# Block-causal attention and FFN on one core: bfloat16 scale sums, leans per operation, and q-high by k-low scores in four 64x64 tiles

## Chip, core and metric

The kernel runs on one NeuronCore of a Trainium2 chip. TensorE (PE) does the matmuls and loads their weights (PEld), VectorE (DVE), ScalarE (ACT) and GpSimd (POOL) work on tiles in SBUF and PSUM, SyncE (SP) issues most of the DMAs and ACT the others. The metric is device time of one execution in microseconds; lower is better.

## The reference, cut

```python
def _attn_ref(q, k, v):                     # 8 batches, 8 heads, 576 tokens, 64 per head, float32
    scores = scale * np.matmul(q, k.transpose(0, 1, 3, 2))
    mask = block_i >= block_j               # blocks of 64 tokens: causal by block
    scores = np.where(mask, scores, -1000000000.0)
    scores = scores - np.max(scores, axis=-1, keepdims=True)
    attn = np.exp(scores)
    attn = attn / (np.sum(attn, axis=-1, keepdims=True) + 1e-09)
    return np.matmul(attn, v).astype(np.float32)

def _moe_ref(x, w_in, w_out):               # x: the heads side by side, 4608 x 512; d_ff 2048
    h = x @ w_in
    g = h * np.clip(h + 3.0, 0.0, 6.0) / 6.0
    return (g @ w_out).astype(np.float32)
```

## The kernel before

**Numbers in two halves.** From batch 1 on, every float32 operand of a matmul is scaled by a power of two and split into two float16 numbers, a high and a low one; a product is then three or four float16 products summed in PSUM. Batch 0 goes through float32 matmuls (names `qt`, `sf`, `pt`, `pr`, `pf`, and `h`, `o` of the first piece), because the weights are still being loaded and split then. The power of two comes from the largest absolute values: `pow2_scale` (L747) sums the 128 partitions' values with a matmul against a column of ones (`mb`, two instructions of 1 or 2 columns, float32), for q and k of each slot, for v of each batch and for five weight chunks (the last two through a transpose `mt` first); three more weight chunks have a sum of their own (`gs`, in `w_max`, L889).

**Slots.** A slot is one pair of heads of one batch; slots 0 to 3 are batch 0, slots 4 to 31 are batches 1 to 7. For a slot `qk_prep` (L1040) takes the absolute maxima `qkmx` (DVE; for the first slots ACT may do it), scales q and k, and lays out `qks` in three slices: q's high and low halves beside each other, k's high half twice, k's low half twice. One transposing DMA makes `qkT` of it: 128 rows, of which 64 are high and 64 low in slice 0.

**Scores.** `s_group` (L1289) computes the scores of three 64-token query blocks of a slot; three groups make the nine blocks. A 64-column tile of PE takes head 0 and the other 64-column tile head 1 (`128*64` in the profile: 128 rows by 64 columns), so instructions come in pairs that run side by side. Each block is two such pairs over its keys: q (high and low) by k high, and q (high and low) by k low. Group 1 has blocks of 256, 320 and 384 columns, each in a PSUM bank of its own; group 2 has 448, 512 and 576 (576 in two pieces, 64 of them beside the 448 in one bank, 512 in another). The score banks are the pool `ps_s`, three of them. After a bank DVE takes the row maxima (`st<-s`), scales them, ACT does the exponential with its sum (`p<-s`), and the result is split (`phl`), transposed by DMA (`pT`) and multiplied with v (`pv`).

**FFN.** Thirteen pieces of tokens go through `h` (w_in, 16 steps of a piece), `r` and `g` (ACT and DVE) and `o` (w_out), with up to four accumulators `o0` to `o3`; the last two pieces use a product with seven instead of eight submatrices (`m`). `ffn2_` (L1671) writes a piece's output tiles `osb` and their DMAs.

**Order.** Nothing is issued directly. A recorder notes every operation with its possible engines, and `schedule` (L474) lays them out with a model of costs, a due time for each and a table `SHIFT` of some 1,450 offsets to due times; `emit` (L677, line L681 in the profile) then issues them, so that all instructions have one line and tiles tell them apart. An operation with several possible engines goes to the one that would end first, with fixed handicaps (`BIAS`: 250 ns for DVE, 500 ns for POOL). PE works in the order it is given; matmuls of one `joint` group stay together.

Of the kernel before, what the change touches and what calls it, by code (L numbers as in the profile page):

```python
# [9 lines left out]
BF16 = mybir.dt.bfloat16  # L10
# [7 lines left out]
P = 128  # L18
# [33 lines left out]
QKA = 8  # L52
RDW = "PA"
# [1881 lines left out]
```

## Time and profile before

| what | us |
|---|---|
| median of 3 runs (992.11 to 992.73) | 992.53 |
| the profiled execution | 993.4 |
| its span on the core | 991.6 |
| PE busy (98%) | 971.2 |
| DVE busy (89%) | 883.6 |
| ACT busy (65%) | 641.9 |
| POOL busy (6%) | 58.7 |

The span runs from the first instruction to the last; 1.8 us of the profiled execution lie around it. Busy time of PE is the union of modelled matmul durations. A matmul's start is recorded, its end is modelled: what a stretch of matmuls costs is read from the start of its first to the start of the next stretch's first. PE's granted clock is full (1.00) throughout.

### The profile page before, as it was taken

How to read it: one execution, taken by the hardware profiler on the slowest of the kernel's cores; microseconds unless marked ns; L12 is line 12 of the kernel's file. 1: busy time of each engine (PE TensorE's matmuls, PEld its weight loads, DVE VectorE, ACT ScalarE, POOL GpSimd, SP SyncE). 2: the span in 40 equal slices, each digit the busy share in tenths (PEclk: the TensorE clock that was granted, in tenths of full speed). 3: DMA queues.
4: the chain of work that ended last, by engine and by line, in shares of the span. 5: the costliest groups of instructions: out<-in, count | busy, mean ns of one | idle time of the engine just before them, and what ended most of it. 6: DMA issues, size and time to landing. Idle time of an engine off the chain costs nothing.

```text
span 991.6 us, 31314 instructions
## 1 busy us (share of the span) xinstructions
PE 971.2 (98%) x12673; PEld 729.3 (74%) x12673; DVE 883.6 (89%) x2443; ACT 641.9 (65%) x1547; POOL 58.7 (6%) x228
## 2 busy tenths in 40 slices
PE   6899999999999999999999999999999999999998
PEld 5565667777768876777777777877777777887876
DVE  6898999999998999999999988898998879985863
ACT  4799777866756767676776656765766554444442
POOL 1132100000000000000000000000000000000000
PEclk9999999999999999999999999999999999999999
DMA  8975567999769999698888887576674452000000
GB/s 237 292 217 162 99 123 144 163 174 203 131 115 182 153 179 164 127 189 158 149 165 151 142 159 119 110 160 119 115 168 88 84 118 23 15 34 2 34 2 33
DMA packets 407041, 129.05 MB, mean 130 GB/s; under 512 B 393968, under 2 KB 396272, under 8 KB 406896
## 3 DMA queue, kind: packets, MB, share of 16 engines
q1 hardware_dynamic: 362816, 113.59, 58.8%
q10 hardware_dynamic: 44080, 13.46, 6.4%
q8 instruction: 99, 1.62, 0.7%
q14 instruction: 46, 0.38, 0.1%
HBM read 45.09 MB, written 9.44 MB: 55 GB/s over the span
## 4 chain that ended last, share of the span: by engine, by line
PE 46%; DVE 3%; ACT 1%; DMA 1%; issue 0%; ACTq 0%; DVEq 0%
PE o L681 21%; PE h L681 14%; PE m L681 6%; PE s L681 3%; PE pv L681 3%; DVE phl L681 1%; DVE st L681 1%; DVE g L681 1%; DMA vnat<-in_v_dram 1%; DVE r L681 0%; ACT p L681 0%; DVE x L681 0%; ACT r L681 0%; ACTq L681 0%; DVE vhl L681 0%
## 5 line engine op out<-in xcount | busy, mean ns | idle before, releaser
L681 PE MATMUL o<-wout,g 128*64 128x512 f16 (+3 forms) x3336 | 404.5, 379 | 0.0
L681 PE MATMUL h<-x,win 128*64 128x384 f16 (+2 forms) x3952 | 361.0, 319 | 2.1 <-DVE r L681 2.0
L681 PEld LDWEIGHTS <-win 128*64 128x64 f16 (+1 forms) x4440 | 271.8, 110 | 57.8 <-issue 4.7
L681 PEld LDWEIGHTS <-g 128*64 128x64 f16 x3360 | 221.6, 110 | 107.8
L681 ACT ACTIVATE p<-s,st,esc 128x64 f32<-128x64 f32 (+1 forms) x280 | 162.9, 587 | 58.9 <-DVE st L681 35.1
L681 ACT ACTIVATE r<-h,eg,sh 128x384 f32<-128x384 f32 (+1 forms) x192 | 111.4, 599 | 62.6 <-PE h L681 58.7
L681 DVE SCALAR_TENSOR_TENSOR phl<-p,st,phl 128x128 f16<-128x128 f32 (+4 forms) x252 | 136.0, 582 | 0.5 <-ACT phl L681 0.5
L681 DVE TENSOR_REDUCE st<-s 128x1 f32<-128x64 f32 (+2 forms) x280 | 117.8, 446 | 11.0 <-PE s L681 10.9
L681 ACT ACTIVATE g<-r 128x384 f16<-128x384 f32 (+1 forms) x153 | 77.7, 509 | 58.8 <-DVE r L681 39.9
L681 DVE SCALAR_TENSOR_TENSOR g<-r,g 128x384 f16<-128x384 f32 (+1 forms) x192 | 101.7, 534 | 13.4 <-ACT g L681 12.5
L681 DVE SCALAR_TENSOR_TENSOR r<-r,eg,h 128x384 f32<-128x384 f32 (+1 forms) x160 | 93.6, 586 | 10.3 <-ACT r L681 9.8
L681 PE MATMUL s<-qkT 128*64 128x512 f16 (+7 forms) x1120 | 96.8, 287 | 0.8 <-ACT p L681 0.3
L681 ACT ACTIVATE phl<-p,st 128x128 f16<-128x128 f32 (+4 forms) x135 | 71.9, 565 | 37.8 <-DVE st L681 23.1
L681 PEld LDWEIGHTS <-vhl 128*64 128x64 f16 x1680 | 72.0, 110 | 11.3 <-issue 3.6
L681 PEld LDWEIGHTS <-qkT 128*64 128x64 f16 x1120 | 59.6, 110 | 24.2 <-issue 5.0
L681 PE MATMUL pv<-pT,vhl 128*64 128x192 f16 (+2 forms) x1680 | 73.0, 233 | 2.3 <-DVE x L681 1.9
L681 ACT ACTIVATION_READ_ACCUMULATOR p<-s,st,esc 128x1 f32 x280 | 55.3, 197 | 0.0
L681 POOL MEMSET p<- 128x64 f32 x140 | 21.3, 152 | 556.0 <-DVE phl L681 519.1
L681 ACT ACTIVATE r<-hf,eg,sh 128x192 f32<-128x192 f32 (+1 forms) x48 | 25.8, 591 | 38.6 <-DVE hf L681 38.6
L681 DVE TENSOR_SCALAR phl<-p,st 128x384 f16<-128x384 f32 (+4 forms) x117 | 45.0, 413 | 1.3
L681 DVE SCALAR_TENSOR_TENSOR qks<-qk,rs_q,qks 128x576 f16<-128x576 f32 x56 | 44.5, 809 | 0.0
L681 PE MATMUL m<-x,ws 128*64 128x192 f16 x768 | 35.4, 246 | 0.0
(191 smaller groups left out, 1023.3 us busy)
## 6 DMA issues: line engine op xcount, KB each, us to landing
out_dram<-osb SPq DMA_DIRECT2D x35, 256.0 KB, 2.4
qk<-in_q_dram SPq DMA_DIRECT2D x23, 288.0 KB, 4.1
rawo<-in_moe_w_out_dram SPq DMA_DIRECT2D x12, 512.0 KB, 4.5
vnat<-in_v_dram ACTq DMA_DIRECT2D x34, 128.0 KB, 3.8
qk<-in_k_dram ACTq DMA_DIRECT2D x14, 288.0 KB, 4.8
qk<-in_k_dram SPq DMA_DIRECT2D x14, 288.0 KB, 4.3
vnat<-in_v_dram SPq DMA_DIRECT2D x30, 128.0 KB, 3.0
x<-in_moe_w_in_dram SPq DMA_DIRECT2D x7, 512.0 KB, 5.7
```

The costliest lines, as they stand in the source:

```text
L681: getattr(eng, method)(*args, **kw)
```

## The change

- **Scale sums.** The columns of ones become bfloat16, and the values summed are read as the upper 16 bits of their float32 words, in `pow2_scale` and `w_max`.
- **Scores in 64x64 tiles.** q's high and low words stand in swapped order in the odd blocks of 128 tokens of `qks`. In group 1 the 320-column block goes first, alone, then the 256- and 384-column blocks as one joint set in two banks; in group 2 the set of two banks stays as it was. In such a set q (high and low) by k high comes first, in 128x64 tiles. Then q high alone by k low, for two blocks and two heads, in four 64x64 tiles: the swap puts the two blocks' high words into different row halves. The product of the two low words is left out there (not in the other regions). Each such stretch, 56 of them, is four instructions.
- **qk_prep.** q's high words come from one instruction over ten blocks instead of nine, its low words from two DVE instructions (five and four blocks) instead of one. ACT may take the maxima `qkmx` in all slots.
- **Order.** `SHIFT` is another table; a new table `LEAN`, some 900 entries, adds to the handicap of DVE and POOL for single operations; POOL's costs in the planner are raised.
- **Small ones.** `rd` in `pv_group32` (batch 0) is one product on DVE or POOL instead of three on POOL or ACT. The last output tile is written in two halves, by ACT and DVE, with a DMA each. (`VMG` is 99, above every slot, so `v_max` is as before.)

```diff
-QKA = 8
-RDW = "PA"
+QKA = 32
+RDW = ("vector", "gpsimd")
+VMG = 99
...
-    0: -10, 2: 71, 3: -67, 4: -29, 5: 85, 6: -33, 7: -5, 8: 114, 11: -102, 12: 63, 13: 4, 14: -6, 15: 14,
...
+            op.lean = self.BIAS
+            if len(ways) > 1:
+                part = self.part[op.grp] = self.part.get(op.grp, -1) + 1
+                dv, dp = LEAN.get(10 * op.grp + part, (0, 0))
+                if dv or dp:
+                    op.lean = dict(vector=self.BIAS["vector"] + dv, gpsimd=self.BIAS["gpsimd"] + dp)
...
+    def upper(a):
+        return a.bitcast(BF16).rearrange("p (n w) -> p n w", w=2)[:, :, 1]
...
-            nc.tensor.matmul(ps[h * BLK:(h + 1) * BLK, :n], ones[:k_, :BLK], mx, start=True, stop=True)
+            nc.tensor.matmul(ps[h * BLK:(h + 1) * BLK, :n], ones[:k_, :BLK], upper(mx), start=True, stop=True)
...
-    one = wpool.tile([P, 1], F32, tag="one", name="one")
+    one = wpool.tile([P, 1], BF16, tag="one", name="one")
...
-        nc.scaled(sp[:, 0, :, 0], t[:, 0], rs[:, 0:1], "AV")
-        nc.scaled(sp[:, 1, :, 0], t[:, 1], rs[:, 1:2], "AV")
-        nc.vector.scalar_tensor_tensor(
-            sp[:, 0, :, 1], t[:, 0], rs[:, 0:1], sp[:, 0, :, 0], op0=ALU.mult, op1=ALU.subtract
-        )
+        nc.scaled(qs[:, :, 0::3], qf, rs[:, 0:1], "AV")
+        nc.scaled(sp[:, 2, :, 0], t[:, 1], rs[:, 1:2], "AV")
+        for u in range(2):
+            nc.vector.scalar_tensor_tensor(
+                sp[:, 0, u::2, 1 - u], t[:, 0, u::2], rs[:, 0:1], sp[:, 0, u::2, u],
+                op0=ALU.mult, op1=ALU.subtract,
+            )
...
-        for i in range(GB):
-            nc.scaled(rd[:, i], ident2, r[:, i:i + 1], RDW)
+        eye, rr = ident2.unsqueeze(1).to_broadcast([P, GB, BLK]), r.unsqueeze(2).to_broadcast([P, GB, BLK])
+        nc.add([(e, "tensor_tensor", (rd, eye, rr), dict(op=ALU.mult)) for e in RDW])
...
-            [[[(ii, 0, BLK * (GB + ii + 1), 0)]] for ii in range(GB)],
+            [[[(1, 0, 320, 0)]], [[(0, 0, 256, 0)], [(2, 0, 384, 0)]]],
...
+            pss = [ps_s.tile([P, 512], F32, tag="s", name=f"s{n}_{g}_{si}_{bi}") for bi in range(len(some))]
+            nc.joint = "s", n, g, si
+            work = []
             for bi, bank in enumerate(some):
...
+                for ii, c0, c1, o in reversed(bank):
+                    work.append((0, bi, ii, c0, c1, o, 2))
+                    work.append((int(len(some) > 1 and o == 0), bi, ii, c0, c1, o, 1))
+            for quad, bi, ii, c0, c1, o, sl in sorted(work, key=lambda x: x[0]):
+                i = g * GB + ii
+                nc.share = 4 if quad else 2
+                for h in range(2):
+                    r = slice(0, P)
+                    if quad:
+                        t_ = (h * NB + i) // 2 % 2
+                        r = slice(t_ * BLK, (t_ + 1) * BLK)
+                    nc.tensor.matmul(
+                        pss[bi][h * BLK:(h + 1) * BLK, o:o + c1 - c0],
+                        T[r, 0, h * S + i * BLK:h * S + (i + 1) * BLK],
+                        T[r, sl, h * S + c0:h * S + c1],
+                        start=(sl == 2), stop=(sl == 1),
+                    )
...
+            if pc == NPC - 1 and t == nt - 1:
+                for h, (e, qu) in enumerate((("A", "scalar"), ("V", "sync"))):
+                    hs = slice(h * DM // 2, (h + 1) * DM // 2)
+                    nc.scaled(o[:, hs], a[:, hs], so[:, t:t + 1], e)
+                    nc.load(rows[:, hs], o[:, hs], (qu,))
```

How the order moves, at three places. On PE, scores of group 1 of a slot of batch 1: before, the 384-column block stands by itself between FFN matmuls (four instructions, each behind its weight load).

```order
L681 MATMUL h_11_736<-x_82,win 64x384
L681 LDWEIGHTS qkT_642
L681 MATMUL s_1_2_0_701<-qkT_642 64x384
...
L681 LDWEIGHTS win
L681 MATMUL h_11_736<-x_82,win 64x384
```

Now, the same slot's joint set; the first pair of each block is q by k high, the second q high by k low.

```order
L847 MATMUL o_1_632<-wout,g_8_695 64x512
L847 LDWEIGHTS qkT_642
L847 MATMUL s_1_1_0_699<-qkT_642 64x256
...
L847 MATMUL s_1_1_1_700<-qkT_642 64x384
...
L847 MATMUL s_1_1_0_699<-qkT_642 64x256
...
L847 MATMUL s_1_1_1_700<-qkT_642 64x384
L847 LDWEIGHTS g_8_695
L847 MATMUL o_2_633<-wout,g_8_695 64x512
```

The 256- and 384-column blocks, which had FFN work between them, now stand next to each other, eight instructions in one set. On PE, the scale sum of the same batch, before:

```order
L681 MATMUL h_3_628<-x_82,win 64x384
L681 MATMUL mb_q_640<-qkmx_635,one 64x2 x2
L681 LDWEIGHTS win
L681 MATMUL h_4_651<-x_82,win 64x384
L681 LDWEIGHTS win
```

And now:

```order
L847 MATMUL h_4_651<-x_82,win 64x384
L847 LDWEIGHTS one
L847 MATMUL mb_q_640<-qkmx_635,one 64x2
L847 LDWEIGHTS one
L847 MATMUL mb_q_640<-qkmx_635,one 64x2
L847 LDWEIGHTS win
```

The bfloat16 sums have weight loads of their own and stand between `h` steps as before. On DVE, q and k of one slot (`qks_636`), before:

```order
L681 SCALAR_TENSOR_TENSOR qks_636<-qk_634,rs_q_638,qks_636 128x9x64
L681 SCALAR_TENSOR_TENSOR phl_0_627<-p_0_624,st_0_622,phl_0_627 128x128
...
L681 SCALAR_TENSOR_TENSOR qks_636<-qk_634,rs_q_638,qks_636 128x9x64
L681 TENSOR_SCALAR st_1_643<-st_1_643,esc_570 128x1
L681 TENSOR_SCALAR qks_636<-qks_636 128x2x9x32
```

And now:

```order
L847 SCALAR_TENSOR_TENSOR qks_636<-qk_634,rs_q_638,qks_636 128x5x64
L847 TENSOR_SCALAR phl_0_627<-p_0_624,st_0_622 128x128
...
L847 SCALAR_TENSOR_TENSOR qks_636<-qk_634,rs_q_638,qks_636 128x4x64
L847 SCALAR_TENSOR_TENSOR qks_636<-qk_634,rs_q_638,qks_636 128x9x64
L847 TENSOR_SCALAR qks_636<-qks_636 128x2x9x32 x2
```

The low words of q take two instructions, and both copies of k stand on DVE here. Counted over the whole program, DVE's maxima `qkmx` fall from 24 to 5 (ACT takes 23 slots, two instructions each), DVE's copies `g` rise from 34 to 51 and its `osb` of 512 columns from 2 to 11; the one-column scalings of `st` fall by 56, the two-column ones rise by 28. Changes of PE's tile shape from one matmul to the next (128x128 with the transposes, 128x64, 64x64, one- and two-row `mb`) are 164 before and 265 now: 112 more at the score sets, 11 fewer elsewhere.

## Rows read from the trace of the kernel before

**Rows 1.** The page's head, its part 1, and PE, DVE and granted clock in 40 slices of the span (tenths).

```profile
span 991.6 us, 31314 instructions
PE 971.2 (98%) x12673; PEld 729.3 (74%) x12673; DVE 883.6 (89%) x2443; ACT 641.9 (65%) x1547; POOL 58.7 (6%) x228
PE   6899999999999999999999999999999999999998
PEclk9999999999999999999999999999999999999999
```

**Rows 2.** Busy time of the engines in stretches of the span: from and to, length, then PE, PEld, DVE, ACT, POOL with their instructions, granted clock, DMA share, GB/s.

```profile
300.00:500.00 200.00, 199.22 (x2824) 152.34 (x2818) 194.00 (x565) 144.36 (x363) 10.03 (x51) 1.00 0.91 163
900.00:987.00 87.00, 87.00 (x1381) 69.98 (x1378) 56.20 (x141) 33.24 (x65) 0.00 (x0) 1.00 0.03 11
```

**Rows 3.** What PE waited for, longest in total: the first two rows from 0 to 140 us, the others after 140 us (total us, times, longest).

```profile
PE qt L681 <- DMA qf<-in_q_dram: 5.2, 2, 4.5
PE sf L681 <- ACT pf L681: 3.2, 3, 2.1
...
PE h L681 <- DVE r L681: 2.0, 2, 1.8
PE pv L681 <- DVE x L681: 1.9, 4, 0.5
```

**Rows 4.** PE in order of time at four score banks (start, duration of the merged row, instructions); the row behind each is the next work. The 448-column row holds four instructions of 448 and four of 64 columns.

```profile
364.94 0.41 PE L681 MATMUL s<-qkT 128*64 128x256 f16 x4
365.18 0.66 PE L681 MATMUL h<-x,win 128*64 128x384 f16 x6
...
321.88 0.52 PE L681 MATMUL s<-qkT 128*64 128x384 f16 x4
322.21 0.94 PE L681 MATMUL h<-x,win 128*64 128x192 f16 x18
322.95 0.62 PE L681 MATMUL s<-qkT 128*64 128x512 f16 x4
323.38 1.39 PE L681 MATMUL o<-wout,g 128*64 128x512 f16 x14
...
351.69 0.63 PE L681 MATMUL s<-qkT 128*64 128x448 f16 x8
352.13 0.69 PE L681 MATMUL h<-x,win 128*64 128x384 f16 x6
```

**Rows 5.** PE in order of time in batch 0: float32 matmuls of 512 columns (each record is one of two passes) in one 128x128 tile, then in four 64x64 tiles, and what follows each.

```profile
77.75 1.88 PE L681 MATMUL o<-wout,g 128*128 128x512 f32 x4
79.56 0.98 PE L681 MATMUL sf<-qkf 64*64 64x384 f32 x8
...
92.31 1.09 PE L681 MATMUL sf<-qkf 64*64 64x512 f32 x8
93.33 0.59 PE L681 MATMUL h<-x,win 128*128 128x192 f32 x2
```

**Rows 6.** PE in order of time around a scale sum of v, whose weights have one row (`1*64`).

```profile
393.48 1.17 PE L681 MATMUL h<-x,win 128*64 128x384 f16 x12
394.58 0.28 PE L681 MATMUL mb_v<-dg_v,one 1*64 1x1 f32 x4
394.79 1.17 PE L681 MATMUL h<-x,win 128*64 128x384 f16 x12
395.79 0.60 PE L681 MATMUL s<-qkT 128*64 128x512 f16 x4
```

**Rows 7.** PE in order of time around two scale sums of q and k (two instructions of two passes each).

```profile
469.80 0.26 PE L681 MATMUL mb_q<-qkmx,one 128*64 128x2 f32 x4
469.88 0.84 PE L681 MATMUL o<-wout,g 128*64 128x512 f16 x6
...
304.45 0.28 PE L681 MATMUL mb_q<-qkmx,one 128*64 128x2 f32 x4
304.59 0.42 PE L681 MATMUL h<-x,win 128*64 128x192 f16 x6
```

**Rows 8.** Groups of DVE and ACT by shape: count, then busy us, mean ns of one, idle us before.

```profile
L681 DVE SCALAR_TENSOR_TENSOR qks<-qk,rs_q,qks 128x576 f16<-128x576 f32 x56 | 44.5, 809 | 0.0
L681 DVE TENSOR_REDUCE qkmx<-qk 128x2 f32<-128x1152 f32 x24 | 32.2, 1343 | 0.0
L681 DVE TENSOR_SCALAR st<-st,esc 128x1 f32<-128x1 f32 x112 | 22.0, 205 | 0.4
L681 DVE TENSOR_SCALAR st<-st,esc 128x2 f32<-128x2 f32 x28 | 6.2, 222 | 0.2
L681 DVE SCALAR_TENSOR_TENSOR phl<-p,st,phl 128x256 f16<-128x256 f32 x56 | 26.8, 478 | 0.5 <-ACT phl L681 0.5
L681 ACT ACTIVATE qks<-qk 128x576 f16<-128x576 f32 x8 | 5.4, 677 | 0.1
L681 ACT ACTIVATE p<-s,st,esc 128x512 f32<-128x512 f32 x56 | 43.4, 774 | 15.1 <-PE h L681 7.5 <-DVE phl L681 3.4 <-DVE st L681 2.2
```

**Rows 9.** The end: the last piece of the chain that ended last (start, us), the half-width `osb` of an earlier piece as a group of ACT, and the output DMAs (KB each, median us from issue to landing).

```profile
987.85 0.69 ACT osb L681
...
L681 ACT ACTIVATE osb<-o,so 128x256 f32<-128x256 f32 x1 | 0.5, 476 | 0.0
...
out_dram<-osb SPq DMA_DIRECT2D x35, 256.0 KB, 2.4
```

More of the change, by code (lines that the diff above doesn't have):

```diff
@@ L78 @@
 SHIFT = {
[154 rows of a table removed]
[154 rows of a table added]
+}
+LEAN = {
[156 rows of a table added]
 }
 class Op:
-    __slots__ = ("ways", "key", "grp", "preds", "joint", "n", "start", "end", "tiles", "eng", "half")
+    __slots__ = ("ways", "key", "grp", "lean", "preds", "joint", "n", "start", "end", "tiles", "eng", "half")
 class Engine:
@@ L277, in __init__ @@
         self.grp = 0
+        self.part = {}
         self.joint = None
@@ L461, in cost @@
                 return 20 + 1.0 * n, 50 + n, False
-            occ = 75 + (2.0 if method == "tensor_tensor" else 1.1) * n
+            occ = 75 + (2.6 if method == "tensor_tensor" else 1.3) * n
             return occ, occ + 30, True
@@ L573, in schedule @@
                         else:
-                            mine = t + ways[e][2] + self.BIAS.get(e, 0.0)
+                            mine = t + ways[e][2] + ops[k].lean.get(e, 0.0)
                             r = min(
-                                max(now[q], ready[k][q]) + ways[q][2] + self.BIAS.get(q, 0.0)
+                                max(now[q], ready[k][q]) + ways[q][2] + ops[k].lean.get(q, 0.0)
                                 for q in ways if q != e
@@ L800 @@
         nc.gpsimd.memset(cross[h * BLK:(h + 1) * BLK, h * BLK:(h + 1) * BLK], 0.0)
-    one = wpool.tile([P, 1], F32, tag="one", name="one")
+    one = wpool.tile([P, 1], BF16, tag="one", name="one")
     nc.gpsimd.memset(one, 1.0 / E_IN)
     ones = one.to_broadcast([P, P])
-    unit = wpool.tile([P, 1], F32, tag="unit", name="unit")
+    unit = wpool.tile([P, 1], BF16, tag="unit", name="unit")
     nc.gpsimd.memset(unit, 1.0)
@@ L919, in w_max @@
         for h in range(2):
-            nc.tensor.matmul(ps2[h * BLK:(h + 1) * BLK, :2], full1, m, start=True, stop=True)
+            nc.tensor.matmul(ps2[h * BLK:(h + 1) * BLK, :2], full1, upper(m), start=True, stop=True)
         nc.joint = None
@@ L996, in v_max @@
         else:
-            absmax(vmax[b][:, hp:hp + 1], vnat[n % NVB], AX.XYZ)
+            ways = [("vector", "tensor_reduce", (vmax[b][:, hp:hp + 1], vnat[n % NVB]),
+                     dict(axis=AX.XYZ, op=ALU.max, apply_absolute_value=True))]
+            if n >= VMG:
+                ab = sm.tile([P, NJ, 2, D], BF16, tag="vs", bufs=1, name=f"va{n}")
+                ways.append(("scalar", "activation", (ab, vnat[n % NVB], AF.Abs),
+                             dict(accum_out=vmax[b][:, hp:hp + 1])))
+            nc.add(ways)
         if hp == NPAIR - 1:
@@ L1046, in qk_prep @@
             ways.append(("scalar", [
-                ("activation", (sp[:, 2].rearrange("p t l d -> p (t l d)")[:, :NST * D].rearrange("p (t d) -> p t d", d=D), t[:, s], AF.Abs), dict(accum_out=mx[:, s:s + 1]))
+                ("activation", (sp[:, 1].rearrange("p t l d -> p (t l d)")[:, :NST * D].rearrange("p (t d) -> p t d", d=D), t[:, s], AF.Abs), dict(accum_out=mx[:, s:s + 1]))
                 for s in range(2)
@@ L1056, in qk_prep @@
         esc[n] = sc
-        nc.scaled(sp[:, 0, :, 0], t[:, 0], rs[:, 0:1], "AV")
-        nc.scaled(sp[:, 1, :, 0], t[:, 1], rs[:, 1:2], "AV")
+        ev = NST + NST % 2
+        qs = sp.rearrange("p c t l d -> p (c t) l d")[:, :ev].rearrange("p (a u) l d -> p a (u l) d", u=2)
+        qf = t.rearrange("p c t d -> p (c t) d")[:, :ev].rearrange("p (a u) d -> p a u d", u=2)
+        nc.scaled(qs[:, :, 0::3], qf, rs[:, 0:1], "AV")
[5 more added lines that the diff above has]
+            )
         nc.vector.scalar_tensor_tensor(
-            sp[:, 0, :, 1], t[:, 0], rs[:, 0:1], sp[:, 0, :, 0], op0=ALU.mult, op1=ALU.subtract
-        )
-        nc.vector.scalar_tensor_tensor(
-            sp[:, 2, :, 0], t[:, 1], rs[:, 1:2], sp[:, 1, :, 0], op0=ALU.mult, op1=ALU.subtract
+            sp[:, 1, :, 0], t[:, 1], rs[:, 1:2], sp[:, 2, :, 0], op0=ALU.mult, op1=ALU.subtract
         )
@@ L1301, in s_group @@
             [[[(0, 0, 64, 0), (1, 0, 128, 64), (2, 0, 192, 192)]]],
-            [[[(ii, 0, BLK * (GB + ii + 1), 0)]] for ii in range(GB)],
[1 row of a table added]
             [[[(1, 0, 512, 0)]], [[(0, 0, 448, 0), (2, 0, 64, 448)], [(2, 64, 576, 0)]]],
         )[g]
-        col = (1, 0, 2) if g == 2 else (0, 1, 2)
+        col = (1, 0, 2) if g else (0, 1, 2)
         st = sm.tile([P, 14], F32, tag="stg", bufs=3, name=f"st{n}_{g}")
@@ L1310, in s_group @@
             regions = []
+            pss = [ps_s.tile([P, 512], F32, tag="s", name=f"s{n}_{g}_{si}_{bi}") for bi in range(len(some))]
+            nc.joint = "s", n, g, si
+            work = []
             for bi, bank in enumerate(some):
-                ps = ps_s.tile([P, 512], F32, tag="s", name=f"s{n}_{g}_{si}_{bi}")
-                nc.joint = "s", n, g, si, bi
-                for ii, c0, c1, o in bank:
-                    i = g * GB + ii
-                    for sl in (1, 2):
-                        for h in range(2):
-                            nc.tensor.matmul(
-                                ps[h * BLK:(h + 1) * BLK, o:o + c1 - c0],
-                                T[:, 0, h * S + i * BLK:h * S + (i + 1) * BLK],
-                                T[:, sl, h * S + c0:h * S + c1],
-                                start=(sl == 1),
-                                stop=(sl == 2),
-                            )
-                nc.joint = None
+                for ii, c0, c1, o in reversed(bank):
[15 more added lines that the diff above has]
+                    )
+            nc.share = 2
+            nc.joint = None
+            for ps, bank in zip(pss, some):
                 for ii, c0, c1, o in bank:
@@ L1331, in s_group @@
             i0, i1 = min(col[x[0]] for x in regions), max(col[x[0]] for x in regions) + 1
-            if len(some) > 1:
+            if g == 2 and si:
                 nc.vector.tensor_tensor(st[:, 2:3], st[:, 2:3], st[:, 3:4], op=ALU.min)
@@ L1730, in ffn2_ @@
                 )
-            else:
+            elif pc < NPC - 1 or t < nt - 1:
                 nc.scaled(oc, ac, so[:, t:t + 1] if pc else 1.0 / 6.0, "AV")
             rows = out[row + t * P:row + t * P + n]
-            if half:
+            if pc == NPC - 1 and t == nt - 1:
[3 more added lines that the diff above has]
+                    nc.load(rows[:, hs], o[:, hs], (qu,))
+            elif half:
                 for h in range(2):
```

463 rows, old and new, of tables (LEAN, SHIFT) are left out of this document.

## Prediction

> **What bounds the kernel now.** I read the page's head first [rows 1]: PE is busy for 971.2 of 991.6 us, at its full clock in every slice, and only the first two slices and the end stand below 9. DVE is at 89%, which is near enough to matter, so the second view is busy time by stretch [rows 2]: from 300 to 500 us PE has 199 of 200 us and DVE 194, while from 900 us on DVE has 56 of 87. The third view, what PE waited for [rows 3], says which of the two ends last: after 140 us PE's two longest waits in total are 2.0 and 1.9 us, and before 140 us 5.2 us go to the first loads (4.5 us of it one wait) and 3.2 to ACT. So PE's own stream sets the time, DVE keeps up just so, and a change is worth what it does to the stream. As busy durations of PE overlap, I price everything from start to start in the order of time.
>
> **Scores in four tiles: what they save.** A pair of 384 columns takes 0.165 us (0.33 us for two), one of 512 columns 0.215 us, which is 2.38 columns per ns; one of 256 columns 0.11 by that rate (the row has 0.24 us for two), and 448 columns 0.19 (0.44 us less two pairs of 64) [rows 4]. In a four-tile stretch the shorter block should run beside the longer: 256 beside 384, 448 beside 512. That saves 0.11 + 0.19 = 0.30 us per slot, 28 slots: **-8.4 us**. That four 64x64 tiles do run at once is seen in batch 0 [rows 5]: four float32 passes of 512 columns in one tile take 1.81 us up to the next work, while eight records of 512 columns in four tiles take 1.02 us, two passes' worth, not eight.
>
> **What they cost.** The same rows show a price for the change of tile shape. A float32 pass of 512 columns takes twice 0.215, 0.43 us; four make 1.72, and the row has 1.81 before the four-tile work starts: 0.09 us to go in. Two passes in four tiles make 0.86, and the next work starts after 1.02: 0.16 us for the weights that couldn't be loaded ahead and for going out [rows 5]. The nearest case in float16 is a scale sum of v, whose weights have one row, so that rows change and columns don't, as with q's halves [rows 6]. Twelve `h` instructions (six pairs of 0.161) should take 0.97 us; ahead of the sum they take 1.10, behind it 1.00, and the sum itself 0.21, against 0.08 to 0.14 for a sum of q and k that keeps the shape [rows 7]. That is 0.13 + 0.03 + 0.10 = 0.26 us for going in and out. For a four-tile stretch I get 0.28 from rows 5 with the 0.03 behind it; a float16 weight load is shorter than a float32 one, so I take 0.25 and keep 0.22 to 0.28. There are 56 stretches, two per slot, and none touches another in the new order: 56 x 0.25 = **+14.0 us** (12.3 to 15.7). So the stretch with 256 and 384 columns loses 0.14 us, the one with 448 and 512 loses 0.06, and the scores alone come out 5.6 us dearer.
>
> The Trainium skill, TensorEngine Tiling (Array Packing), section Key Properties, says that changing the tiling mode, not merely the tile, drains the TensorE. Rows 6 agree, with about 0.13 us a change; a reader who goes by that page's table of speedups alone would book the 8.4 us and no more.
>
> **Other changes of shape.** Elsewhere the new order has 11 changes fewer, at half of 0.25 each: **-1.4 us** (0 to -1.5).
>
> **Scale sums.** A float32 sum of q and k takes 0.08 to 0.14 us in the stream, say 0.10 [rows 7]; with one pass in place of two it can't fall below the 0.03 us that the smallest pair needs (the 64-column pairs in rows 4, by the rate): 28 x 0.07 = 2.0. The 16 sums of v and of weights lose one of two passes, some 0.06 us each of the 0.21 in rows 6, and keep their change of shape: 1.0. Together **-3.0 us** (-1 to -4). The Trainium skill, TensorEngine Tiling (Array Packing), section Instruction Overhead, gives about 60 cycles to any matmul however few its columns; as an estimate two would take 0.05 us one after the other, and the first 2.0 would be 1.4. No row here has a bfloat16 sum.
>
> **The end.** The last `osb` takes ACT 0.69 us; half of it took 0.48, and the DMA behind it, 2.4 us for 256 KB, becomes two of 128 KB [rows 9]: **-0.3 us** (-0.2 to -0.6).
>
> **Work off PE.** DVE loses 19 maxima of 1.343 us (-25.5) and, by merging the scalings of `st`, 56 x 0.205 - 28 x 0.222 = -5.3; it gains 28 times the difference between two short residuals (0.48 for 256 columns and 0.54 for 320, between the rows) and one of 0.81, +6; and 26 copies and `osb` of at most 0.81 each, +21 at most [rows 8]. In sum -25 to -4 us of 883.6: I cost this at nothing, since PE ends last, and what it could give is bounded by PE's waits. ACT gains 38 passes of 0.677 us and sheds copies; at 65% busy this is hidden behind PE. If that cover went, a late maximum would hold back `qkT`, and with it a slot's scores, but the planner has FFN work ahead of them. The `rd` products of batch 0 (12 instructions for 36) are within this.
>
> **The tables.** They reorder everything, with no operation added. What they can give is PE's waits: 3.9 us in the start beyond the 4.5 of the first load, and 3.9 later [rows 3]. What they can take has no row; I set the same, 8 us, as the other end. I take 0.
>
> **Sum.** -8.4 + 14.0 - 1.4 - 3.0 - 0.3 = +0.9 us on the profiled execution of 993.4, that is 994.3. That execution lies 0.9 us above the median of the runs, 992.53, so the median I forecast is **993.4 us**, +0.1%. A measurement of this kernel can tell about 0.2%, 2 us; this is no change.
>
> **Rivals.**
>
> *The changes of shape cost little (faster).* If going between 128x64 and 64x64 in float16 let the weights be loaded ahead, a stretch would pay only the 0.03 us of rows 6: 1.7 in place of 14.0, sum -11.4, about 981 us. For it: no row has float16 in 64x64 tiles. Against it: rows 5 and 6 show the price with either type and with rows alone changing. Chance 0.13.
>
> *The order removes waits (faster).* DVE is relieved where it was fullest, by up to 25 us, and the leans allow a finer choice of engine. If half to two thirds of the 7.8 us of waits go, with the rest of the sum as above, it is 988 to 989 us. For it: PE waits for DVE and ACT both in the start and later [rows 3]. Against it: these waits are few, and the start is filled with loads. Chance 0.22.
>
> *The joint set waits for banks (slower).* A set needs two of the three score banks before its first instruction, and in group 1 the banks were taken one by one before. PE takes instructions in order, so when the second bank is still being read, everything behind the set waits too, `h` and `o` included, and then `r` and `g` on ACT and DVE starve. The reader is an exponential of 0.774 us for 512 columns [rows 8]; a set that meets it waits half of it on the mean, 0.39 us. From five such sets in 56 on it decides (2 us); with one in three, 19 x 0.39 = 7.4 us, about 1000.5 us. For it: DVE at 97% in the middle returns banks late. Against it: PE waits for `s` banks hardly at all now, and the planner asks for room before it places a set. Chance 0.19, and 0.08 more for a forecast that holds in kind with the dear ends of the terms (+15.7, sums -1, other changes 0), 996 to 997 us.
>
> **Chances.** The forecast within 0.2%: 0.38. Faster: 0.13 + 0.22 = 0.35. Slower: 0.19 + 0.08 = 0.27. Most chance lies on no single side; the forecast's own range, from the bounds of its terms, is 990 to 997. For eight in ten the range goes down past the second rival and most of the way into the third: 985 to 999; the first rival and the third at its full price stay outside.
>
> **What would show it.** In the profile of the changed kernel: four `s` records of 64x64 starting within 0.03 us of each other, and the next work 0.16 + 0.12 us (384 columns) or 0.215 + 0.12 us (512) after them, with some 0.1 us between the last 128x64 pair's own time and the first of the four; `mb_q` in about 0.03 us from start to start; `qkmx` on ACT; waits of PE for `s` banks under 1 us in total. The prediction is wrong if the four-tile stretches follow the stream without a gap, if PE shows waits of several us behind `s`, or if the waits of the start have gone.

## The result, and the profile after

| kernel | median us | ratio to before, 95% interval |
|---|---|---|
| before, in the same series | 992.32 (990.68 to 993.72) | |
| changed | 1000.71 (999.76 to 1002.59) | 1.0089 [1.0078, 1.01] |

The change is slower by 8.4 us, and above the range of 985 to 999. The profiled execution took 1001.37 us, its span is 998.5. The page's head and its part 1, which answer to [rows 1]:

```profile
span 998.5 us, 31136 instructions
PE 972.2 (97%) x12585; PEld 657.4 (66%) x12585; DVE 882.9 (88%) x2471; ACT 649.0 (65%) x1574; POOL 45.8 (5%) x207
```

The span grew by 6.9 us, PE's busy time by 1.0 (972.2 against 971.2), so 5.9 us are time in which PE stood. (The two profiled executions differ by 8.0 us; the 1.1 us left lie outside the spans, and no run here says why.) Where it stood, the busy time by stretch says (columns as in [rows 2]), first of the changed kernel:

```profile
0.00:200.00 200.00, 186.68 (x2020) 124.96 (x2022) 181.03 (x536) 146.99 (x371) 17.16 (x60) 1.00 0.74 176
200.00:240.00 40.00, 33.49 (x420) 21.02 (x416) 36.96 (x108) 23.99 (x62) 1.46 (x9) 0.91 0.76 151
300.00:500.00 200.00, 197.91 (x2726) 131.99 (x2724) 183.62 (x540) 141.22 (x358) 7.71 (x45) 1.00 0.86 149
```

and of the kernel before, in the first two of these stretches:

```profile
0.00:200.00 200.00, 186.80 (x2046) 127.67 (x2046) 181.06 (x533) 151.78 (x395) 31.41 (x82) 1.00 0.75 179
200.00:240.00 40.00, 39.56 (x526) 29.75 (x528) 39.96 (x111) 27.49 (x65) 1.92 (x11) 1.00 0.97 187
```

Up to 200 us PE stands as long as before (13.3 and 13.2 us): the waits of the start have not gone. From 200 to 240 us it stands 6.5 us against 0.4: all of the 5.9 us. In the middle DVE is indeed relieved, 183.6 us of 200 against 194.0. What PE waited for after 140 us (as in [rows 3]):

```profile
PE mb_q L847 <- ACT p L847: 5.4, 2, 5.3
```

One wait of 5.3 us, a scale sum behind an exponential. Here is the place in the order of time (start, duration of the merged row, then the idle time before it and what ended it); first PE, then DVE, ACT and SP's queue:

```profile
216.50 0.81 PE L847 MATMUL o_2b<-wout,g 128*64 128x512 f16 x6
217.15 0.99 PE L847 MATMUL s<-qkT 128*64 128x192 f16 x16
218.37 0.85 PE L847 MATMUL pv<-pT,vhl 128*64 128x192 f16 x18 [0.22 <-DMA pT<-phl]
224.49 0.22 PE L847 MATMUL mb_q<-qkmx,one 128*64 128x2 bf16 x2 [5.27 <-ACT p L847]
224.95 2.25 PE L847 MATMUL s<-qkT 128*64 128x512 f16 x12 [0.25 <-DVE am_q L847]
...
217.39 0.74 DVE L847 SCALAR_TENSOR_TENSOR osb<-o_2b,so,x 128x512 f32<-128x512 f32 x1
219.58 2.20 DVE L847 SCALAR_TENSOR_TENSOR phl<-p,st,phl 128x512 f16<-128x512 f32 x3
221.71 1.07 DVE L847 TENSOR_REDUCE st<-s 128x1 f32<-128x64 f32 x4
...
223.01 0.41 ACT L847 ACTIVATE p<-s,st,esc 128x64 f32<-128x64 f32 x1 [2.10 <-DVE st L847]
224.93 0.50 ACT L847 ACTIVATE x<-pv 128x384 f16<-128x384 f32 x1
...
206.53 6.04 SPq L847 DMA_TRANSPOSE qkT<-qks  x1
```

The same work of the kernel before:

```profile
212.70 0.75 PE L681 MATMUL s<-qkT 128*64 128x64 f16 x16
213.26 0.68 PE L681 MATMUL h<-x,win 128*64 128x384 f16 x6
213.74 0.84 PE L681 MATMUL o_0b<-wout,g 128*64 128x512 f16 x6
...
214.73 1.49 PE L681 MATMUL o_0b<-wout,g 128*64 128x512 f16 x12
...
222.28 0.84 PE L681 MATMUL o_2b<-wout,g 128*64 128x512 f16 x6
...
217.74 0.39 ACT L681 ACTIVATE p<-s,st,esc 128x64 f32<-128x64 f32 x1
218.56 0.48 ACT L681 ACTIVATE x<-pv 128x384 f16<-128x384 f32 x1
...
198.72 5.76 SPq L681 DMA_TRANSPOSE qkT<-qks  x1
```

Compare one latency with and without cover, that is, with and without other work for PE beside it. Slot 8's first scores are exponentiated 5.0 us after PE began them before (212.70 to 217.74), and 5.9 us now (217.15 to 223.01). Before, PE filled that time with `h` and `o`: the last `o` of piece 1 stands at 222.28. Now piece 1 is done first, at 216.50, and the scores come behind it. The DMA that makes slot 8's `qkT` goes out at 206.53, not 198.72, but PE shows no wait for it at 217.15: what put the last `o` ahead of the scores is the order that PE was given. `h` of piece 2 needs the second half of slot 7's `x`, which ACT copies at 224.93 (218.56 before). The scale sum takes a bank of the pool `ps_s`, as scores and `pv` do; the three are full (slot 8's first two score banks and `pv`'s), and what empties the first of them, ACT's `p`, waits for DVE's maxima, which stand behind `osb` of piece 1 and `phl`. PE has 0.85 us of `pv` to do and then stands. Behind the wait the clock is at half:

```profile
219.00:224.49 5.49, 0.22 (x9) 0.08 (x3) 4.77 (x13) 3.36 (x12) 0.55 (x3) 0.75 0.69 161
224.49:228.35 3.86, 3.61 (x22) 1.72 (x23) 3.78 (x16) 1.33 (x5) 0.15 (x1) 0.50 0.47 90
```

Now the terms of the sum. Score sets and scale sums of the changed kernel, each with the next work behind it (answers to [rows 4, 6, 7]); the row at 360.13 is the four-tile stretch of the set above it, by itself:

```profile
358.09 0.17 PE L847 MATMUL mb_q<-qkmx,one 128*64 128x2 bf16 x2
358.12 1.15 PE L847 MATMUL h<-x,win 128*64 128x384 f16 x12
...
359.76 0.73 PE L847 MATMUL s<-qkT 128*64 128x256 f16 x8
360.13 0.36 PE L847 MATMUL s<-qkT 64*64 64x256 f16 x4
360.42 1.17 PE L847 MATMUL h<-x,win 128*64 128x384 f16 x12
...
370.57 0.97 PE L847 MATMUL s<-qkT 128*64 128x64 f16 x12
371.48 0.68 PE L847 MATMUL h<-x,win 128*64 128x384 f16 x6
...
378.39 0.19 PE L847 MATMUL mb_v<-dg_v,one 1*64 1x1 bf16 x2
378.50 0.84 PE L847 MATMUL o<-wout,g 128*64 128x512 f16 x6
```

The set of 256 and 384 columns takes 0.66 us (eight instructions, four of them in four tiles); before, its blocks took 0.24 + 0.33 = 0.57. Its parts are 0.11 + 0.165 for q by k high and 0.165 for the longer block of the four tiles: 0.22 is left as the price of the two changes of shape. The set of 448, 64 and 512 columns takes 0.91 (0.44 + 0.43 before); less 0.06 for the 64 columns, 0.19 + 0.215 and 0.215, 0.23 is left. The row at 360.13 says where it goes: the four-tile stretch begins 0.37 us after the set, 0.10 more than 0.11 + 0.165, and the next work 0.29 us later, 0.12 more than 0.165. So four tiles do run side by side (four instructions, two of 256 and two of 384 columns, within 0.36 us), and the price is 0.22 to 0.23 a stretch, where 0.25 was forecast. A sum of q and k takes 0.03 us (0.08 to 0.14 in [rows 7]), a sum of v 0.11 (0.21 in [rows 6]).

The end, the last pieces of the chain that ended last:

```profile
994.91 0.48 ACT osb L847
...
995.41 0.48 DVE osb L847
```

The two halves of the last tile run one after the other, not at once.

### The profile page after: what moved, and what is told of

It reads as the page before. It is cut to its first block, busy times and chain, and to the rows that moved or that the text cites. A ratio compares the mean times of both kernels' runs of the same rounds, so it can differ in the third digit from the quotient of the medians.

```text
span 998.5 us, 31136 instructions
## 1 busy us (share of the span) xinstructions
PE 972.2 (97%) x12585; PEld 657.4 (66%) x12585; DVE 882.9 (88%) x2471; ACT 649.0 (65%) x1574; POOL 45.8 (5%) x207
## 4 chain that ended last, share of the span: by engine, by line
PE 57%; DVE 3%; ACT 1%; ACTq 0%; issue 0%; DMA 0%; DVEq 0%
PE o L847 25%; PE h L847 19%; PE m L847 6%; PE s L847 4%; PE pv L847 4%; DVE phl L847 1%; ACT p L847 1%; DVE st L847 1%; ACTq L847 0%; DMA pT<-phl 0%; DVE r L847 0%; DVE g L847 0%; DVE vhl L847 0%; ACT r L847 0%; DVE qks L847 0%
## 5 line engine op out<-in xcount | busy, mean ns | idle before, releaser
L847 PE MATMUL o<-wout,g 128*64 128x512 f16 (+2 forms) x3336 | 405.3, 379 | 0.2 <-ACT osb L847 0.2
L847 PEld LDWEIGHTS <-win 128*64 128x64 f16 (+1 forms) x4440 | 241.0, 110 | 96.2 <-issue 11.2
L847 PEld LDWEIGHTS <-g 128*64 128x64 f16 x3360 | 196.7, 110 | 128.2 <-issue 3.6
L847 ACT ACTIVATE p<-s,st,esc 128x384 f32<-128x384 f32 (+3 forms) x280 | 162.9, 588 | 54.9 <-DVE st L847 40.8
L847 DVE TENSOR_REDUCE st<-s 128x1 f32<-128x64 f32 (+3 forms) x280 | 115.6, 448 | 7.4 <-PE s L847 6.9
L847 PE MATMUL s<-qkT 128*64 128x512 f16 (+9 forms) x1120 | 89.6, 293 | 0.9 <-ACT p L847 0.4
L847 ACT ACTIVATE phl<-p,st 128x256 f16<-128x256 f32 (+4 forms) x127 | 69.4, 577 | 19.9 <-DVE st L847 11.2
L847 PEld LDWEIGHTS <-vhl 128*64 128x64 f16 x1680 | 70.2, 110 | 13.2 <-issue 2.8
L847 PEld LDWEIGHTS <-qkT 128*64 128x64 f16 (+1 forms) x1120 | 45.4, 109 | 37.6 <-issue 22.2
L847 DVE TENSOR_SCALAR phl<-p,st 128x512 f16<-128x512 f32 (+4 forms) x125 | 47.1, 406 | 2.6
L847 DVE SCALAR_TENSOR_TENSOR qks<-qk,rs_q,qks 128x320 f16<-128x320 f32 (+2 forms) x84 | 47.7, 609 | 0.0
```

Source lines behind the costliest of these rows:

```text
L847: getattr(eng, method)(*args, **kw)
```

## The experiments

Ratios are to the kernel before, run on the same chip in the same series. Over the series its median lies between 991.92 and 992.69 us, so a difference between runs of two series carries up to 0.8 us of that.

**Wide tiles, the order kept.** The second pair of each block keeps its row half of 64 removed: q high and low by k low, in 128x64 tiles; the product of the low words is back.

```diff
-                    if quad:
-                        t_ = (h * NB + i) // 2 % 2
-                        r = slice(t_ * BLK, (t_ + 1) * BLK)
```

> The changed kernel in its own order, instruction for instruction; only the 56 stretches of q high by k low run in 128x64 tiles (q high and low by k low, pair by pair) instead of four 64x64 tiles. Theory (the four-tile stretches cost what the prediction said, +14.0 - 8.4 = +5.6 us, and the 5.3 us wait at 219 us is another matter): 995 us (994 to 996.5), and the wait at 219 us is still there, over 4 us long. Rival A (four tiles save time, the loss lies elsewhere): 1002 us or more. Rival B (the four-tile stretches also bring the wait): the wait goes, 986 to 989 us.

997.3 us, ratio 1.0046 [1.0033, 1.0059]: 3.4 us below the changed kernel. That is the four tiles' cost, above the theory's range (994 to 996.5) and outside both rivals'. Its page's head, and the set of 256 and 384 columns:

```profile
span 994.8 us, 31136 instructions
PE 966.7 (97%) x12585; PEld 704.8 (71%) x12585; DVE 881.7 (89%) x2471; ACT 649.1 (65%) x1574; POOL 46.3 (5%) x207
...
358.43 0.74 PE L847 MATMUL s<-qkT 128*64 128x256 f16 x8
358.97 1.17 PE L847 MATMUL h<-x,win 128*64 128x384 f16 x12
```

The set takes 0.54 us in place of 0.66. Most of the loss is still there, and so is the wait: `mb_q` behind ACT's `p`, 4.9 us in total, 4.0 at once. The four tiles are not the cause of the wait.

**The sums alone.** The kernel before with the columns of ones in bfloat16 and the upper halves of the words; the planner's cost of such a sum is kept, so that the order stays as it was.

```diff
-            nc.tensor.matmul(ps[h * BLK:(h + 1) * BLK, :n], ones[:k_, :BLK], mx, start=True, stop=True)
+            nc.tensor.matmul(ps[h * BLK:(h + 1) * BLK, :n], ones[:k_, :BLK], upper(mx), start=True, stop=True)
...
-    one = wpool.tile([P, 1], F32, tag="one", name="one")
+    one = wpool.tile([P, 1], BF16, tag="one", name="one")
...
-        f32 = mybir.dt.size(ins[0].dtype) == 4
+        f32 = mybir.dt.size(ins[0].dtype) == 4 or n <= 2
```

> The kernel before in its own order; only the scale sums are bfloat16 (one pass in place of two). Theory (PE's stream sets the time, so what a sum gives up comes off the end): -3.0 us, 989.3 us (988.5 to 990.5). Rival (PE waits at the next place for what it was early for): 992 us, no change.

990.05 us against 992.51, ratio 0.998 [0.9969, 0.9991]: -2.5 us, and the fastest kernel of this study. Its page's head:

```profile
span 988.4 us, 31123 instructions
PE 968.4 (98%) x12585; PEld 726.3 (73%) x12585; DVE 883.1 (89%) x2443; ACT 642.0 (65%) x1547; POOL 58.6 (6%) x228
```

and a sum with the next work, in the order of time:

```profile
302.00 0.19 PE L681 MATMUL mb_q<-qkmx,one 128*64 128x2 bf16 x2
302.02 0.44 PE L681 MATMUL h<-x,win 128*64 128x192 f16 x6
```

PE's busy time fell by 2.8 us, nearly the forecast's 3.0.

**The old table.** The changed kernel's operations, with the `SHIFT` of before and an empty `LEAN`. The entries go by the operations' numbers, which the change shifts, so this is a table made for another list.

```diff
-LEAN = {
...
+LEAN = {}
```

> The changed kernel's operations, planned anew with the table of due times of the kernel before and no leans. Theory (the new tables make the wait at 219 us): no wait of PE over 2 us after 140 us, 992 us - 3.0 (sums) + 5.6 (four tiles) - 1.4 (other changes of shape) = 993 to 996 us. Rival (the new operations leave PE short of work where piece 1 of the FFN ends and piece 2 begins, whatever the table): waits of several us between 200 and 240 us again, 1000 us or more. The old table was not made for these operations, so a slow run says only that the place is tight, not that the new table is innocent.

1025.39 us, ratio 1.033 [1.031, 1.035]; after 140 us the waits are of the same kind, and more:

```profile
PE mb_q L690 <- ACT p L690: 4.7, 1, 4.7
PE pv L690 <- ACT p L690: 3.8, 2, 3.4
```

The two longest end at 233.85 and 242.49 us, behind the last `o` of piece 1 (227.64): PE is short of work at the same place under either table. There are other losses, so the 33 us are not this place alone: up to 140 us PE has 122.9 us of work, against 128.3 in the changed kernel. The theory's 993 to 996 us failed and the rival's bounds were met. As the expectation says, that does not clear the new table, since the old one was made for other operations.

**Work in the wait.** The changed kernel with 44 matmuls of 512 columns, whose result nobody reads, ahead of the scale sum that waits, so that PE is busy there and its clock stays up.

```diff
+            if o.n == 1536:
+                for _ in range(22):
+                    for h in range(2):
+                        self.nc.tensor.matmul(outs[h], w[:, :BLK], w, start=True, stop=True)
```

> The changed kernel with 44 more matmuls of 512 columns (22 pairs, about 4.7 us) put ahead of the scale sum that waits 5.3 us at 219 us; they write a bank that is not in use then and is overwritten later. Theory (the granted clock fell because PE stood idle, and the work behind the wait ran at half speed for that): PE's clock stays full, the stretch from 224.5 to 228.3 us takes half the time, 1.5 to 2.0 us off the end: 999 us. Rival (what follows the wait is set by DVE's chain, not by PE's speed): the clock stays full and the end is the same, 1000.7 us within 0.5. Rival B (the clock fell for another reason): half clock again, same time.

1001.38 us, ratio 1.0095 [1.0082, 1.0108]: no gain on 1000.71. A second run of it beside the changed kernel itself:

> busy_wait once more: the clock was full behind the wait, and from the milestone at 206 us (a twentieth piece of FFN work before the wait) to the end it took 1.8 us less than the changed kernel, but its start was 4 us later, part of it under a half clock near 35 us. Theory (half clock behind the wait costs 1.8 us; the start was chance): 1.5 to 2 us under after_again from that milestone to the end, and in the medians if the starts agree. Rival (the clock costs nothing here): the same from milestone to end.

> The changed kernel itself on the chip of this set, so that the others stand beside it: 1000.7 us (999.8 to 1002.6), the wait of 5.3 us at 219 us and half clock behind it again in the profiled execution. Rival (the wait was a chance of one execution): a profile without it.

1000.37 us (999.75 to 1003.44) against 1001.88 (1000.23 to 1004.42) for the changed kernel. The clock did stay at 1.00 from 200 to 240 us. Ahead of the added matmuls `pv` waited 2.1 us for a DMA (`pT`), behind them `h` 1.2 us for DVE's `r`. From the same amount of feed-forward work near 206 us to the last matmul the two profiled executions with the added matmuls took 786.2 and 786.7 us, those of the changed kernel 788.0 and 787.5: 0.8 to 1.8 us less, and the medians don't separate them. So by these traces the half clock costs 1.8 us at most; more closely they don't tell it, since other waits moved too. The stall itself returned in the repeat of the changed kernel (4.8 us in total, longest 3.9), so it is no accident of one execution.

**Another order, long.** The recorded operations planned at 188 to 264 us in another order, written out, so that PE has work at the place of the wait; the DMAs don't keep their old order.

```diff
-        for o in self.schedule():
+        order = self.schedule()
+        byn = {o.n: o for o in order}
+        at = min(i for i, o in enumerate(order) if o.n in set(ORDER))
+        order[at:at + len(ORDER)] = [byn[n] for n in ORDER]
+        for o in order:
```

> The changed kernel, its operations and their engines untouched; only the order of 494 operations that lie between some 188 and 264 us is another one, a fixed list. On PE two steps of h of piece 2 and the pv of slot 7 come ahead of slot 8's first scores, the scale sum comes behind them, and some o of piece 1 later; on DVE the second half of x from slot 7 comes 20 places earlier, the maxima of slot 8's scores 4 to 6, a maximum of v 42 places later. Theory (the wait at 219 us is a fault of the order at that one place; PE and DVE have enough other work to do there): the wait falls under 1 us, the clock stays full, 6 to 9 us come off the end: 992 to 995 us. Rival (DVE and ACT cannot deliver slot 7 and 8 earlier, or what is late there comes back as other waits by 300 us): 998.5 us or more.

> The same fixed list, and besides q high by k low in 128x64 tiles as in wide_tiles. Theory (the two losses are separate, 6 to 9 us and some 3.5 us): 988.5 to 991 us, faster than the kernel before. Rival (with the wait gone the shorter stream of wide_tiles only runs into DVE): as order_moved, 992 us or more.

1007.08 us, ratio 1.0144 [1.0124, 1.0164], and with wide tiles 1005.27, 1.0121 [1.01, 1.0142]: both slower than in the planner's order. Compared at the same amount of feed-forward matmuls done, PE was 3.6 us ahead of the changed kernel near 232 us, although `pv` had waited 2.7 us for `pT`, and 8.9 behind it near 300 us. In between it waited 1.7 us for `qkT`, and at 282 us the scale sum's wait behind `p` was back with 5.6 us. This order had moved the stall further on; the theory failed here.

**Another order, short.** Operations planned at 188 to 235 us alone, 103 moved, the order among the DMAs kept; the lines are those above with another list.

> The changed kernel, its operations and engines untouched; the order of 248 operations between some 193 and 237 us is another, 103 of them stand elsewhere, most by one to five places; the order of the DMAs and all that comes behind stays, which order_moved did not keep. On PE the last steps of o of piece 1 come 2 to 8 places earlier, and three steps of h of piece 2 that can run without the late part of x come 8 to 15 places later, into the gap; on DVE the four maxima of slot 8's scores come up to 3, the second half of x from slot 7 4 places earlier, a maximum of v 42 later. Theory (the wait is partly a fault of the order: the chain of slot 7 and 8 on DVE, ACT and the DMA queue sets the rest): PE's waits from 210 to 232 us fall by 3 to 4 us, and as no wait is long the clock stays full, 1.8 us more: 995 to 997 us in the median, no loss behind it by 300 us. Rival (what is gained comes back behind it, as with order_moved): 1000 us or more.

> As order_short, and q high by k low in 128x64 tiles as in wide_tiles. Theory (the two losses are separate, each known by now: 3.5 us for the tiles, 4 to 6 for the wait): 991 to 993.5 us, level with the kernel before. Rival (one of them hides the other): 995 us or more.

998.63 us, ratio 1.0064 [1.0045, 1.0083], and with wide tiles 996.23, 1.0036 [1.0022, 1.005]. The scale sum's wait fell to 0.3 us, and the next in line showed:

```profile
222.41 0.85 PE L871 MATMUL pv<-pT,vhl 128*64 128x192 f16 x18 [2.98 <-DMA pT<-phl]
223.58 0.19 PE L871 MATMUL mb_q<-qkmx,one 128*64 128x2 bf16 x2 [0.32 <-ACT p L871]
```

That is a gain of 2.1 us with four tiles and 1.1 with wide ones, less than the theories expected (995 to 997, and 991 to 993.5); the 1.1 is not clear of noise, and with wide tiles the scale sum still waited 2.9 us. PE's wait passed on to what was late beside it, here the DMA that makes `pT`.

**Another order, begun earlier.** Operations planned at 148 to 235 us, 238 moved.

> The changed kernel with a written-out order for the stretch planned at 148 to 235 us, 70 us longer than in order_short: 238 recorded operations stand in other places, the scale sum of slot 7, the scores of slots 6 and 7 and with them the qkT of slots 7 and 8 stand ahead of feed-forward work of piece 1, and x of slot 7 is copied ahead of DVE's and ACT's work on piece 2. No operation is added or left out; the order among the DMAs of SP is kept. Theory (the new order runs the feed-forward work of piece 1 ahead of the attention of slots 7 to 9, and PE then stands at the change from piece 1 to piece 2): the qkT of slot 8 goes out 3 to 4 us earlier than the 206.5 us of the changed kernel, no wait of PE above 2.5 us is left between 206 and 236 us, and the kernel takes 993 to 997 us, 4 to 8 us under the changed kernel. Rival (VectorE, ScalarE and the DMAs can't deliver earlier, or the time returns as a wait further on): 998.5 us or more, as order_short with 998.63.

> The same written-out order, with the scores of q high by k low of all batches in 128-row tiles as before the change (one block after the other), as in wide_tiles; the bfloat16 scale sums stay. Theory: 989 to 993 us, 4 to 8 us under wide_tiles (997.3), so that with the stall gone the sums alone are left of the change and it is no slower than the kernel before. Rival: 996 us or more, as order_short_wide with 996.23.

996.41 us, ratio 1.0044 [1.0031, 1.0056], and with wide tiles 992.13, ratio 0.9998 [0.9989, 1.0007]. Both lie within the theories' bounds, though `qkT` of slot 8 goes out only 1.2 us earlier (205.35) in place of 3 to 4. The stretch of `order_early`, busy time by stretch:

```profile
200.00:240.00 40.00, 36.11 (x474) 23.52 (x470) 39.36 (x115) 27.79 (x68) 1.93 (x11) 1.00 0.77 157
```

and PE at the place, in the order of time:

```profile
214.00 0.53 PE L890 MATMUL s<-qkT 128*64 128x192 f16 x12 [0.27 <-DMA qkT<-qks]
214.37 2.12 PE L890 MATMUL h<-x,win 128*64 128x384 f16 x24
...
217.84 0.85 PE L890 MATMUL pv<-pT,vhl 128*64 128x192 f16 x18 [0.74 <-DMA pT<-phl]
220.33 0.19 PE L890 MATMUL mb_q<-qkmx,one 128*64 128x2 bf16 x2 [1.64 <-ACT p L890]
```

The scores of slot 8 stand at 214.00 with 2 us of `h` behind them, the longest wait is 1.64 us, the clock is full, and DVE has 39.4 us of work in the stretch where it had 37.0. PE stands 3.9 us there, not 6.5. No operation was added or removed: the order alone is worth 4.3 us with four tiles (1000.71 to 996.41) and 5.2 with wide ones (997.3 to 992.13). The head of `order_early_wide`:

```profile
span 989.4 us, 31132 instructions
PE 964.9 (98%) x12585; PEld 700.4 (71%) x12585; DVE 881.9 (89%) x2471; ACT 648.8 (66%) x1574; POOL 45.7 (5%) x207
```

Against the sums alone PE has 3.5 us less to do (964.9 against 968.4), both at full clock, and stands 4.5 us longer (24.5 against 20.0 of its span). From 200 to 240 us it still stands 4.6 us. So the stall is smaller, not gone.

## Why the prediction failed

**The tables: the step that failed.** What the new order could take was booked at 0, with 8 us to either side as a bound. Wide tiles and bfloat16 sums in the changed kernel's order take 997.3 us, the sums alone in the old order 990.05. These 7.3 us are what all the rest of the change costs together; no run has the new order without the other edits. By the heads of the two profiled executions PE stands 28.1 us in the one and 20.0 in the other, 8.1 more, while its work does not grow (966.7 and 968.4 us). How much of this is the order is shown in part: the same operations in another order come back by 4.3 to 5.2 us, most of it at the change from piece 1 to piece 2. Whether the table or the operations made the planner's order is not separable, since a table fits one list of operations. Some 2 us are left in the best order tried (992.13 against 990.05), with 4.6 us of waits at the same place; whether a better order removes them stays open.

The prediction looked for waits already in the trace, which an order could remove, and for PE alone; it did not ask which work stands beside a latency that was covered. That question had an answer in the trace of before: scores wait 5 us for their exponentials, with `h` and `o` of piece 1 behind them. And it had a rival for an order that removes waits, but none for an order that makes one.

**The range.** Its upper end is too low by the text's own terms. The dear ends (-8.4 + 15.7, sums -1, other changes 0, the end -0.2) add up to +6.1 us, which is 998.6 us and not 996 to 997; and 8 us for the tables on top of 993.4 alone give 1001.4. The measured 1000.71 lies within that bound, but no chance was set aside for it.

**Four tiles, +5.6 (-8.4 and +14.0).** The mechanism was right and the size a little large: 0.22 to 0.23 a stretch by the rows in place of 0.25. The two sets shown cost 0.09 + 0.04 = 0.13 us a slot more than before, 3.6 us for 28 slots; the runs give 3.4 (997.3 to 1000.71) and 4.3 (992.13 to 996.41). Four tiles lose here because 0.22 us a stretch is more than the 0.11 and 0.19 us that running side by side saves. The Trainium skill, TensorEngine Tiling (Array Packing), section Key Properties, says that a change of the tiling mode drains the TensorE. The 0.10 us before a stretch and the 0.12 after it agree.

**Scale sums, -3.0.** Right: -2.5 us in the runs, -2.8 in PE's busy time. A sum of q and k takes the 0.03 us that the term took as its floor.

**The end, -0.3.** Half of it. From PE's last matmul to the end of the span it is 3.6 us (994.88 to 998.5) against 3.8 before (987.83 to 991.6): the halves' DMAs are shorter (1.7 us from issue to landing, against 2.4 in [rows 9]), but DVE's half began only when ACT's had ended.

**Other changes of shape, -1.4.** Not tried by itself, and so not shown. The term is one of the edits within the 7.3 us. The 3.5 us that PE's work shrank from the sums alone to `order_early_wide` leave room for it, but hold other edits too, such as the blocks of group 1 set side by side (0.54 us in place of 0.24 + 0.33).

**Work off PE, 0.** DVE as a whole lost 0.7 us, not 4 to 25: the copies that it took over weigh about as much as the maxima that it gave up. In the middle PE hides what happens on DVE; at one place it does not. The text had named a price, a late maximum that holds back scores, and trusted that feed-forward work stands ahead of them. At 217 us there was none left; what was late there is not `qkmx` but the maxima of the scores (`st`), and through them the exponentials.

**The rivals.** Cheap changes of shape fell by the 0.22 us. The order that removes waits fell: it brought one. The joint set that waits for banks came nearest in time, 1000.5, by luck and not by its mechanism: `s` waits 0.4 us in total for ACT's `p`, and the bank wait of 5.3 us is a scale sum's, once, behind a latency that lost its cover.

## What to carry to other kernels

When a change re-plans the order, don't price only the waits that are there: list the long latencies that are covered now (scores to exponential, issue to landing) and see in the new order what stands beside each, above all where one piece of work ends and the next depends on late data. Test another order by moving work well ahead of the wait, DVE's and ACT's too: here that gave 4.3 to 5.2 us, while a move at the wait itself gave 1.1 to 2.1, the next late data taking over, and the long list, in which the DMAs lost their old order, cost 6.4 to 8.0. An edit that is good by itself, as the sums are here, is best run alone in the old order before it is shipped with a new one.

## What the runs showed of the chip

- Behind a wait of 5.3 us of PE its granted clock was 0.50, which is 1.2 GHz, for the next 3.9 us; with matmuls in the wait it stayed at 1.00, 2.4 GHz, and from 206 us to the last matmul the kernel took 0.8 to 1.8 us less.
- Going from 128x64 into 64x64 tiles and back cost 0.10 + 0.12 us in float16, while four 64x64 tiles did run side by side.
- The two bfloat16 instructions of a scale sum, two columns each and one in either column half, cost 0.02 to 0.03 us from start to start in a stream of float16 matmuls, though the profile models 0.17 to 0.19 us for them.
